# Windowed attention and a softplus feed-forward layer on one core: scores and transposes on four array tiles, the global-row picks on eight

## The chip, the cores and the metric

The kernel runs on one core of one Trainium2 chip. The metric is the device time of one execution in microseconds (us); lower is better. A core has a matrix engine (PE, with its weight loads shown apart as PEld), a vector engine (DVE), an activation engine (ACT), a general engine (POOL) and a queue engine (SP). POOL and SP also issue DMA transfers.

## The reference

```python
def _attn_ref(q, k, v, global_idx):            # q, k, v: (8, 8, 576, 64); 8 global positions
    scores = scale * np.matmul(q, k.transpose(0, 1, 3, 2))
    mask = np.abs(pos[:, None] - pos[None, :]) <= 32
    mask = mask | is_global[:, None] | is_global[None, :]
    scores = np.where(mask, scores, -1000000000.0)
    attn = softmax(scores)
    return np.matmul(attn, v)

def _moe_ref(x, w_in, w_out):                  # x: (4608, 512), d_ff 2048
    h = x @ w_in
    return softplus(h) @ w_out
```

Eight batches of eight heads with 576 positions and 64 elements a head. Each position attends to a band of 32 positions on either side and to eight global positions; the global positions attend to everything. The attention's output goes through two dense layers with a softplus between them. Inputs and outputs are float32; the kernel computes in bfloat16 with float32 sums.

## The kernel before

**Order.** Nothing runs in the order of the text. Every piece of work is a job with a cost per engine, dependencies, a rank, and the PSUM banks and buffers that it opens (`o.add`). `_Order.run` places the jobs one after another by the time at which they could start, by rank and by number, and then emits them in that order; the engines' queues follow it. It prices a change of the array's form on PE with 95 ns (`SWITCH`). `KINDS` says how many PSUM tiles of a kind may be open and how many banks must be left over, `SLOTS` the same for SBUF buffers; `OPENING` and `LATER` shift ranks by the job's name. There are eight PSUM banks.

**Loads.** `load_qk` brings q or k of one batch into 72 partitions of `qn` or `kn`, each partition with eight consecutive positions of all heads. Batch 0 is brought in parts. A later batch's load waits for the turns and picks of the batch before (`add_load`).

**Preparation of a batch** (`add_prep`). Turns: `tk` and `tq` (L533, L544) transpose 72x64 pieces on two column tiles of the array, 16 transposes for a pair of heads. `kev` and `qev` copy the results from PSUM to `kx` and `qx`. From batch 1 on, `qx` holds each head's 64 columns beside 64 columns of zeros, so `qev` makes two copies and POOL clears the zeros once (`blanks_q`). Picks: `pick` (L491) gathers the eight global rows of k and of q by matmuls with a 0/1 matrix, four 32-column tiles at once, `keep` copies them, `turn` (L502) transposes them, `fill` and `gev` copy them to `kx` and `qg`.

**Scores** (`add_scores`). A unit is 64 queries of one batch, all eight heads, nine units a batch. `sc` makes a unit's scores in two jobs of two head pairs; from batch 1 on each is a full-array matmul over both heads of a pair, thanks to the zeros (L662); in batch 0 there are two 64x64 matmuls for a pair (L667). `top` (DVE, L673) adds the mask and finds the row's minimum of the negated scores.

**Softmax and values.** `ex` (ACT) exponentiates, `su` (DVE) sums, `no` (POOL, L710) normalises to `pn`, `gc` (L714) writes the global columns' weights to `gw`. `pn` is transposed by PE (`tp`) or, for most units, by a DMA transpose on SP (`pt`). `add_global` computes the global rows (`sg`, `mx`, `gexp`, `gsum`, `tg`, `lge`, `ov`, `oz`). `add_values` makes four units' outputs at once: eight or more matmuls on 64x64 tiles for the global keys (L775), 32 for the band (L785), and `xev` copies them out.

**Dense layers** (`add_moe`). 512 tokens make a tile: 16 x 4 matmuls `first` (L819), softplus on ACT, 4 x 16 matmuls `second` (L830), copies and stores.

Of the kernel before, what the change touches and what calls it, by code (L numbers as in the profile page):

```python
# [18 lines left out]
class _Order:  # L19
# [30 lines left out]

    def closed(self, key):
        if key is None:
            return 0
        ends = [u["end"] for u in self.users[key]]
        return None if None in ends else max(ends) + self.HOP

    def room(self, opens):

        t0 = 0
        want = 0  # L60
        spare = 0
        for pool, key in opens:
            cap = self.slots.get(pool) or self.kinds[pool][0]
            was = self.opened[pool]
            if len(was) >= cap:
                t = self.closed(was[-cap])
                if t is None:
                    return None
                t0 = max(t0, t)
            if pool in self.kinds:  # L70
                want += 1
                spare = self.kinds[pool][1]
# [7 lines left out]
    def run(self, free):  # L80
# [16 lines left out]
        while ready:  # L97
            best = None
            for j in ready:
# [8 lines left out]
                for e in j["cost"]:  # L108
                    t = max(t0, free[e])
                    rank = j["rank"]  # L110
                    if e == "PE" and array != 128:
                        rank = 0 if j["array"] == array else rank + 1
# [23 lines left out]
            if e == "PE" and j["array"] != array:  # L136
                array = j["array"]
                t += self.SWITCH
# [34 lines left out]
def kernel(  # L173
# [67 lines left out]

    def load_qk(b, which, h0=0, h1=H):
# [3 lines left out]
    Q_PARTS = ((0, 0, 32), (32, G, NQ - 32))  # L246
# [15 lines left out]
    load_qk(0, 1, H // 2, H)  # L262
# [25 lines left out]
    posQ2 = temp([P, QR], FP32, "posQ2")  # L288
    count(posQ2[0:G, :], [[1, QR]], 0, QR)
    count(posQ2[G:P, :], [[1, QR]], 32 * QR, QR)  # L290
    pick_w = const([P, QR, 32], BF16, "pick")
    pick_0 = const([P, QR, 32], BF16, "pick0")
# [7 lines left out]
    qx = [const([P, HP, NJ, 2, G], BF16, f"qx{i}") for i in range(2)]  # L300
# [8 lines left out]
    def blanks_q(i):  # L309
        def edges():  # L310
            nc.gpsimd.memset(kx[i][:, :, 0, 0:WIN].bitcast(I32), 0)
            nc.gpsimd.memset(kx[i][:, :, NH5 - 1, G - WIN:G].bitcast(I32), 0)
            clear(nc.gpsimd, qg[i][:])
        return [edges] + [lambda p=p, h=h: nc.gpsimd.memset(qx[i][h * D:(h + 1) * D, p, :, 1 - h, :].bitcast(I32), 0)
                          for p in range(HP) for h in range(2)]
# [13 lines left out]
    for lo, at, n in Q_PARTS:  # L329
        nc.gpsimd.dma_start(out=qn[at:at + n, :, :],  # L330
                            in_=q[0].rearrange("h (q r) d -> q h (r d)", r=QR)[lo:lo + n])
# [50 lines left out]
    def ones_g(i):  # L382
# [3 lines left out]
        for p in range(1, HP):  # L386
            nc.vector.tensor_copy(gw[i][:, :, p, 0:2 * NG], gw[i][:, :, 0, 0:2 * NG])
# [22 lines left out]
    ST, PEB, PNB, PTB, RB = 10, 5, 8, 12, 2  # L410
    SLOTS = dict(xT=2, osb=2, st=ST, pe=PEB, pn=PNB, pt=PTB, R=RB, small=2, gk=2)
    for c in range(KF):
        SLOTS[f"g{c}"] = 1

    KINDS = dict(h=(4, 2), o=(3, 1), s=(2, 0), pick=(2, 0), gt=(1, 2), tk=(4, 0), tq=(4, 2), tk0=(1, 0), tq0=(2, 0),
                 sg=(2, 1), tg=(2, 1), ov=(1, 1), tp=(2, 0), rt=(3, 0), xo=(4, 1))
# [37 lines left out]
    def add_load(b, which, deps):  # L454
# [6 lines left out]
        early = [T.get(("t" + "qk"[which] + z, b - 1, p)) for p in range(HP) for z in ("", "b")]  # L461
        early += [T.get(("pick", b - 1, x)) for x in range(2)]
        if b:
            T["load", b, which] = [o.add({"POOL": (880, 0)}, lambda e: load_qk(b, which), deps + early, rank=0, moves=4300)]
# [9 lines left out]
    def add_prep(b, gate, rank):  # L474
# [4 lines left out]
        if b < 2:  # L479
            blanks["g"] = [T["edges", 0] if b == 0 else T["blank_q", 1]]  # L480
        XN = (qn, kn)

        def pick(e, w):
# [3 lines left out]
            parts = ((pick_w, 0, NQ),) if b or w else tuple((pick_0, at, n) for lo, at, n in Q_PARTS)  # L487
# [21 lines left out]
        def gev(e):  # L509
            for h in range(2):  # L510
                r = slice(h * D, (h + 1) * D)
                copy(e, qg[i][r, :, h * NG:(h + 1) * NG], PS["gt", b][r, 0, :, 0:NG])
        for n, w in enumerate((1, 0)):
            T["pick", b, n] = o.add({"PE": (460 * (1 if b or w else 2), 530 * (1 if b or w else 2))}, lambda e, w=w: pick(e, w),
# [12 lines left out]
        plain = qx[0][:].rearrange("c p j h q -> c p (j h q)")[:, :, 0:S]  # L527
        for p in range(HP):
# [18 lines left out]

            def kev(e, p=p):
# [7 lines left out]
            def qev(e, z=0, p=p, parts=parts):  # L556
                lo, at, n = parts[z]
                t = PS["tq", b, p, z][:].rearrange("c r (j q) -> c j q r", q=G // QR)
                if b == 0:
                    copy(e, plain[:, p, lo * QR:(lo + n) * QR].rearrange("c (j q r) -> c j q r", q=G // QR, r=QR), t)  # L560
                    return
                for h in range(2):
                    c = slice(h * D, (h + 1) * D)
                    copy(e, qx[i][c, p, :, h, :].rearrange("c j (q r) -> c j q r", r=QR), t[c])
            T["tk", b, p] = o.add(mm(QR, NQ), tk, [T["load", b, 1][b == 0 and p >= HP // 2], *gate], rank=rank, opens=[("tk" if b else "tk0", ("tk", b, p))], array=64)
            T["kev", b, p] = o.add({"ACT": (635, 720), "DVE": (800, 880)}, kev, [T["tk", b, p], *late, *blanks["g"]],
                                   rank=3, uses=[("tk", b, p)])
            for z, (lo, at, n) in enumerate(parts):
                key = ("tq", b, p, z)
                T["tqb" if z else "tq", b, p] = o.add(mm(QR, n), lambda e, z=z, f=tq: f(e, z), [T["load", b, 0][z], *gate], rank=rank + z,  # L570
                                                      opens=[("tq" if b else "tq0", key)], array=64)
                n = QR * n
                T["qevb" if z else "qev", b, p] = o.add({"ACT": act(n), "DVE": (90 + 1.2 * n, 170 + 1.2 * n)} if b == 0 else {"ACT": (1270, 1370), "DVE": (1530, 1600)},
                                                        lambda e, z=z, f=qev: f(e, z), [T["tqb" if z else "tq", b, p], *late], rank=3 + z, uses=[key])

        if b == 0:
            T["pick", 0, 1]["deps"] += [T["tqb", 0, HP - 1], T["make_pick"]]
# [3 lines left out]
    def add_global(b, gate, early):  # L581
# [24 lines left out]
        def gsum(e):  # L606
# [3 lines left out]
            nc.vector.scalar_tensor_tensor(out=rv[i][:, 0:2], in0=selg[:, 0, :], scalar=rv[i][:, 2:3], in1=selg[:, 1, :],  # L610
                                           op0=OP.mult, op1=OP.add)
# [27 lines left out]
        T["gsum", b] = o.add({"DVE": (530, 630)}, gsum, [T["gexp", b], T["select"], T.get(("oz", b - 2))], rank=2)  # L639
# [9 lines left out]
    def add_scores(n, gate, rank):  # L649
# [3 lines left out]
        def sc(e, x):  # L653
            if x == 0:
                PS["st", n] = sb.tile([P, HP, EXT], FP32, tag="st", name="st", bufs=ST)
                PS["nb", n] = sb.tile([P, HP], FP32, tag="nb", name="nb", bufs=ST)
            kf = kx[i][:].rearrange("c p a w -> c p (a w)")
            ps = PS["s", n, x] = psum(("s", n, x), [P, 2, EXT], FP32)
            for y in range(2):
                p = x * 2 + y  # L660
                if b:
                    nc.tensor.matmul(out=ps[:, y, :], lhsT=qx[i][:, p, j, :, :].rearrange("c h q -> c (h q)"),  # L662
                                     rhs=kf[:, p, j * W:j * W + EXT], start=True, stop=True)
                    continue
                for h in range(2):
                    r = slice(h * D, (h + 1) * D)
                    nc.tensor.matmul(out=ps[r, y, :], lhsT=qx[0][:].rearrange("c p j h q -> c p (j h q)")[r, p, j * G:(j + 1) * G],  # L667
                                     rhs=kf[r, p, j * W:j * W + EXT], start=True, stop=True)

        def top(e, x):  # L670
            for y in range(2):
                p = x * 2 + y
                nc.vector.tensor_tensor_reduce(out=PS["st", n][:, p, :], in0=PS["s", n, x][:, y, :], in1=mask[:, j, :],  # L673
# [372 lines left out]
```

## Time and profile before

| what | value |
|---|---|
| median of 3 runs | 372.06 us (371.8 to 889.26) |
| the profiled execution | 371.55 us, span 369.8 us |
| PE busy | 350.3 us (95% of the span) |
| DVE, ACT, POOL busy | 239.5, 277.2, 153.4 us |
| instructions | 10736 |
| granted PE clock, mean | 1.000 |

The span runs from the first to the last instruction that the profiler recorded; the execution's own time is 1.75 us longer. "Busy" counts the time in which an engine had an instruction under way. PE's matmuls are pipelined, so their records overlap: how long a group really holds PE is read from the difference between its start and that of the next group.

### The profile page before, as it was taken

Reading aid. Unit: us, or ns where it says so; the run is one execution under the profiler, and the core shown is the slowest. Engines: PE = TensorE matmul, PEld = TensorE weight load, DVE = VectorE, ACT = ScalarE, POOL = GpSimd, SP = SyncE. Lnnn points to the kernel's source line nnn. Section 1 sums busy time; section 2 is a strip of 40 time slices with the busy share of each in tenths; the row PEclk is TensorE's granted clock in tenths of the full one; section 3 lists DMA queues with packets and bytes.
Section 4 is the critical chain, followed back from the end, with each engine's and each line's share of the span. In section 5 each row is a group of like instructions: output and inputs, shape, how many; then the busy total and the mean of one; then the engine's idle time right before and its main releaser. Section 6 shows DMA issues by size and latency. Waiting matters only on the chain.

```text
span 369.8 us, 10736 instructions
## 1 busy us (share of the span) xinstructions
PE 350.3 (95%) x4044; PEld 194.3 (53%) x4044; DVE 239.5 (65%) x1028; ACT 277.2 (75%) x724; POOL 153.4 (41%) x258
## 2 busy tenths in 40 slices
PE   1977999999999999999999999999999999999996
PEld 0744777465545554555455545544554455445444
DVE  5689758996679756975697569755975595163011
ACT  3695898997599759885988598959895986784710
POOL 8988820691038503940295029502840180060000
PEclk9999999999999999999999999999999999999999
DMA  6999993099319981698159916980692022021002
GB/s 95 153 234 188 195 168 61 31 104 176 88 44 144 153 156 45 130 144 166 40 132 122 183 40 139 139 170 31 143 107 76 29 87 59 1 73 58 0 30 85
DMA packets 86164, 38.99 MB, mean 105 GB/s; under 512 B 68064, under 2 KB 79584, under 8 KB 86112
## 3 DMA queue, kind: packets, MB, share of 16 engines
q0 software_dynamic: 53248, 18.37, 46.8%
q1 hardware_dynamic: 32864, 19.94, 23.7%
q8 instruction: 31, 0.51, 0.6%
q14 instruction: 21, 0.17, 0.2%
HBM read 36.71 MB, written 9.44 MB: 125 GB/s over the span
## 4 chain that ended last, share of the span: by engine, by line
PE 68%; DVE 15%; ACT 7%; DMA 4%; issue 3%; POOL 3%; DVEq 0%; POOLq 0%; ACTq 0%
PE h L819 34%; PE o L830 16%; DVE sm L702 6%; PE s L662 4%; PE xo L785 3%; ACT pe L694 2%; PE tq L544 2%; DMA qn<-in_q_dram 2%; DVE rs L704 2%; PE pick L491 2%; DVE rs L703 2%; PE tk L533 2%; DVE osb L448 2%; PE xo L775 1%; ACT L602 1%
## 5 line engine op out<-in xcount | busy, mean ns | idle before, releaser
L710 POOL TENSOR_TENSOR pn<-pe,rs 128x512 bf16<-128x512 f32 x72 | 74.7, 1039 | 169.5 <-DVE rs L704 134.4
L819 PE MATMUL h<-xT,win 128*128 128x512 bf16 (+1 forms) x640 | 138.8, 361 | 0.1
L830 PE MATMUL o<-wout,g 128*128 128x512 bf16 (+1 forms) x592 | 136.2, 374 | 0.0
L825 ACT ACTIVATE g<-h 128x512 bf16<-128x512 f32 (+1 forms) x160 | 86.0, 558 | 41.9 <-PE h L819 40.9
L673 DVE CUSTOM_DVE_ANT_0 st<-s,mask 128x136 f32<-128x136 f32 x288 | 69.8, 295 | 45.3 <-PE s L662 43.8
L694 ACT ACTIVATE pe<-st,nb 128x136 f32<-128x136 f32 x288 | 92.1, 403 | 0.8 <-DVE nb L673 0.7
L819 PEld LDWEIGHTS <-win 128*128 128x128 bf16 x640 | 60.1, 99 | 50.9 <-issue 2.0
L830 PEld LDWEIGHTS <-g 128*128 128x128 bf16 x592 | 55.1, 98 | 57.2 <-issue 3.3
L702 DVE TENSOR_REDUCE sm<-pe 128x4 f32<-128x544 f32 x63 | 44.8, 711 | 10.0 <-ACT pe L694 9.8
L448 DVE COPY osb<-o 128x512 f32<-128x512 f32 (+1 forms) x26 | 17.3, 664 | 28.2 <-PE o L830 28.1
L251 POOL DMA_DIRECT2D vA<-in_v_dram x40 | 34.3, 874 | 0.0
L448 DVE COPY qx<-tq 64x576 bf16<-64x576 bf16 (+2 forms) x35 | 25.5, 728 | 5.6 <-PE tq L544 5.0
L662 PEld LDWEIGHTS <-qx 128*128 128x128 bf16 x252 | 20.5, 98 | 14.2 <-issue 0.3
L662 PE MATMUL s<-kx,qx 128*128 128x136 bf16 x252 | 26.9, 223 | 0.0
L673 DVE DVE_READ_ACCUMULATOR2_ANT nb<- 128x1 f32 x288 | 23.8, 83 | 0.0
L448 ACT CAST xT<-xo 128x512 bf16<-128x512 f32 x19 | 10.9, 590 | 12.1 <-PE xo L785 12.1
L533 PE MATMUL tk<-ident_b,kn 72*64 72x72 bf16 x512 | 13.5, 205 | 6.2 <-DMA kn<-in_k_dram 6.2
L448 ACT COPY kx<-tk 128x32 bf16<-128x32 bf16 (+1 forms) x75 | 18.0, 359 | 1.9 <-PE tk L533 1.8
L704 DVE TENSOR_TENSOR rs<-rs,notg 128x4 f32<-128x4 f32 x72 | 17.7, 246 | 2.5
L448 ACT COPY qx<-tq 64x576 bf16<-64x576 bf16 (+2 forms) x29 | 17.2, 593 | 1.9 <-PE tq L544 1.6
L714 POOL TENSOR_TENSOR gw<-pe,rs 128x32 bf16<-128x32 f32 x72 | 17.2, 238 | 3.0 <-DVE rs L704 1.8
L703 DVE RECIPROCAL rs<-sm 128x4 f32<-128x4 f32 x72 | 12.7, 177 | 6.5
(113 smaller groups left out, 347.5 us busy)
## 6 DMA issues: line engine op xcount, KB each, us to landing
out_dram<-osb SPq DMA_DIRECT2D x35, 256.0 KB, 2.2
vB<-vA SPq DMA_DIRECT2D x16, 256.0 KB, 7.0
kn<-in_k_dram POOLq DMA_DIRECT2D x7, 576.0 KB, 12.1
qn<-in_q_dram POOLq DMA_DIRECT2D x7, 576.0 KB, 14.6
vA<-in_v_dram POOLq DMA_DIRECT2D x24, 128.0 KB, 6.4
win<-in_moe_w_in_dram POOLq DMA_DIRECT2D x2, 1024.0 KB, 15.6
wout<-in_moe_w_out_dram POOLq DMA_DIRECT2D x4, 512.0 KB, 10.7
vA<-in_v_dram POOLq DMA_DIRECT2D x16, 96.0 KB, 5.2
```

Of the source, the lines that this page charges most:

```text
L251: nc.gpsimd.dma_start(out=vA[b % 2][p0:p0 + hi - lo, t, :].rearrange("p (h d) -> p h d", h=H), in_=SRC[2][b, :, lo:hi, :].rearrange("h s d ...
L448: (nc.scalar.copy if e == "ACT" else nc.vector.tensor_copy)(out, in_)
L533: nc.tensor.transpose(out=ps[h * D:(h + 1) * D, r, :], in_=kn[0:NQ, p * 2 + h, r * D:(r + 1) * D], identity=ident_b[0:NQ, 0:NQ])
L662: nc.tensor.matmul(out=ps[:, y, :], lhsT=qx[i][:, p, j, :, :].rearrange("c h q -> c (h q)"), rhs=kf[:, p, j * W:j * W + EXT], start=True, ...
L673: nc.vector.tensor_tensor_reduce(out=PS["st", n][:, p, :], in0=PS["s", n, x][:, y, :], in1=mask[:, j, :], scale=-SCALE, scalar=3.0e38, op0 ...
L694: nc.scalar.activation(out=pe[:, p, 0:EXT], in_=PS["st", n][:, p, :], func=AF.Exp, bias=PS["nb", n][:, p:p + 1], scale=-1.0, **({"accum_ou ...
L702: nc.vector.reduce_sum(out=sm[:], in_=PS["pe", n][:, :, 0:EXT], axis=AX)
L704: nc.vector.tensor_tensor(out=rs[:], in0=rs[:], in1=notg[:, j:j + 1].to_broadcast([P, HP]), op=OP.mult)
L710: nc.gpsimd.tensor_tensor(out=pn[:].rearrange("c p (a s) -> c p a s", a=2), in0=wide[:, :, :, 0:G], in1=rs[:].unsqueeze(2).unsqueeze(3).to ...
L819: nc.tensor.matmul(out=h[:, :], lhsT=w_in_t[c * P // WC][:, kd, c * P % WC:c * P % WC + P], rhs=PS["xT", m][:, kd, lo:hi], start=(kd == 0) ...
L825: nc.scalar.activation(out=PS["g", m, c][:, lo:hi], in_=PS[key][:, :], func=AF.Softplus)
L830: nc.tensor.matmul(out=PS[key][:, :], lhsT=PS["g", m, kf][:, ns * P:(ns + 1) * P], rhs=w_out_t[kf // 4][:, kf % 4, lo:hi], start=(kf == 0) ...
```

## The change

- Scores from batch 1 on are no longer full-array matmuls with zeros. Every unit has eight 64x64 matmuls that address four tiles of the array, and three units make one job, which opens four PSUM banks. `qx` loses its zeros, and POOL its memsets. In odd head pairs the two heads' halves of the partitions are swapped, and `gw`, `rv` and the value matmuls follow.
- From batch 1 on q and k lie in one buffer `nq`, k in partitions 0 to 63 and q in 64 to 127: eight slices of 512 positions and a ninth with the last 64. Each is loaded by two transfers (`load_main`, `load_rest`), and all four wait for every turn and pick of the batch before. One turn job (`tkq`) transposes q and k of two head pairs with 72 transposes on four tiles and opens four banks; there are two such jobs a batch.
- The picks of q and k from batch 1 on are one job of 24 matmuls on eight 64x32 tiles.
- Batch 0 loads q by heads instead of by rows, so its turns of q are whole.
- A value job may run its global part first or last, so that it meets the array's form before it.
- `gsum` makes two small operations of one. Buffers (`ST`, `PTB`), `KINDS` and the ranks are new.

```diff
+    def enters(self, j, array):
+        return 64 if j.get("both") and array == 64 else j["array"]
...
+    nq = const([P, H, (QR + 1) * D], BF16, "nq")
+    def load_main(b, which):
+        nc.gpsimd.dma_start(out=nq[(1 - which) * G:(2 - which) * G, :, 0:QR * D],
+                            in_=SRC[which][b, :, 0:G * QR].rearrange("h (q r) d -> q h (r d)", r=QR))
+    def load_rest(b, which):
+        nc.gpsimd.dma_start(out=nq[(1 - which) * G:(2 - which) * G, :, QR * D:], in_=SRC[which][b, :, G * QR:].rearrange("h q d -> q h d"))
...
-    qx = [const([P, HP, NJ, 2, G], BF16, f"qx{i}") for i in range(2)]
+    qx = [const([P, HP, S], BF16, f"qx{i}") for i in range(2)]
...
-    ST, PEB, PNB, PTB, RB = 10, 5, 8, 12, 2
+    ST, PEB, PNB, PTB, RB = 12, 5, 8, 14, 2
...
-    KINDS = dict(h=(4, 2), o=(3, 1), s=(2, 0), pick=(2, 0), gt=(1, 2), tk=(4, 0), tq=(4, 2), tk0=(1, 0), tq0=(2, 0),
-                 sg=(2, 1), tg=(2, 1), ov=(1, 1), tp=(2, 0), rt=(3, 0), xo=(4, 1))
+    KINDS = dict(h=(4, 0), o=(4, 0), s=(4, 0), pick=(4, 0), gt=(1, 2), tk=(2, 0), tq=(3, 2), tk0=(1, 0), tq0=(3, 1),
+                 sg=(3, 0), tg=(1, 1), ov=(1, 0), tp=(4, 1), rt=(4, 1), xo=(4, 1))
...
-        if b:
-            T["load", b, which] = [o.add({"POOL": (880, 0)}, lambda e: load_qk(b, which), deps + early, rank=0, moves=4300)]
+        early += [T.get(("tk", b - 1, p)) for p in range(HP) if b > 1]
+        early += [T.get(("pick", b - 1, x)) for x in range(2) if b > 1]
+        T["load", b, which] = [o.add({"POOL": (880, 0)}, lambda e: load_main(b, which), deps + early, rank=0, moves=3900),
+                               o.add({"POOL": (850, 0)}, lambda e: load_rest(b, which), deps + early, rank=0, moves=1000)]
...
+        def pick_both(e):
+            for r in range(QR + 4):
+                g = r % 4
+                for w in range(2):
+                    rows = slice((1 - w) * G, (2 - w) * G)
+                    hs = slice(0, H) if r < QR else slice(g * 2, g * 2 + 2)
+                    x = min(r, QR)
+                    nc.tensor.matmul(out=PS["pick", b, w][g * 32:(g + 1) * 32, hs, :], lhsT=pick_b[rows, x, :],
+                                     rhs=nq[rows, hs, x * D:(x + 1) * D], start=(r < 4), stop=(r >= QR))
...
+            def tkq(e, p=p):
+                for r in range(QR + 1):
+                    for w, ps in ((1, PS["tk", b, p]), (0, PS["tq", b, p, 0])):
+                        rows = slice((1 - w) * G, (2 - w) * G)
+                        for h in range(2):
+                            nc.tensor.transpose(out=ps[h * D:(h + 1) * D, r, :], in_=nq[rows, p * 2 + h, r * D:(r + 1) * D],
+                                                identity=ident_b[rows, rows])
...
-            nc.vector.scalar_tensor_tensor(out=rv[i][:, 0:2], in0=selg[:, 0, :], scalar=rv[i][:, 2:3], in1=selg[:, 1, :],
-                                           op0=OP.mult, op1=OP.add)
+            for y in range(2):
+                nc.vector.tensor_scalar(out=rv[i][:, y:y + 1], in0=rv[i][:, 2:3], scalar1=selg[:, 0, y:y + 1],
+                                        scalar2=selg[:, 1, y:y + 1], op0=OP.mult, op1=OP.add)
...
-                if b:
-                    nc.tensor.matmul(out=ps[:, y, :], lhsT=qx[i][:, p, j, :, :].rearrange("c h q -> c (h q)"),
-                                     rhs=kf[:, p, j * W:j * W + EXT], start=True, stop=True)
                 for h in range(2):
                     r = slice(h * D, (h + 1) * D)
+                    for y in range(2):
+                        c = slice((h ^ y) * G, (h ^ y) * G + G)
+                        ps, at = PS["s", u, x * 2 + y]
+                        nc.tensor.matmul(out=ps[c, at, :], lhsT=qx[i][r, x * 2 + y, ju * G:(ju + 1) * G],
+                                         rhs=kf[r, x * 2 + y, ju * W:ju * W + EXT], start=True, stop=True)
...
+        units = [n] if b == 0 else [n - j % 3 + u for u in range(3)]
...
-    OPENING = dict(blank_w=-2, first=0.5, no=0.5, oev=2, ones_g=-2, sec=4.5, su=2.5, w_in=1, w_out=-4)
-    LATER = dict(first=2, gc=-1, kev=-8, oev=-0.5, pick=2, qev=1, re=2, sec=1, sg=3, su=1.5, top=-0.5, w_out=-4)
+    OPENING = dict(gc=-5, pt=2.5, softh=4, su=2.5, top=2.5, w_out=-5)
+    LATER = dict(blank_w=-0.5, ex=-0.5, lge=3, mx=2, pick=4, qev=2, re=2.5, sc=-1.5, su=2.5, tk=-1, tp=-2, w_out=-6)
```

## The prediction

> **What bounds the kernel now.** I read the page first: spans, the slices and the chain that ended last.
>
> ```profile
> span 369.8 us, 10736 instructions
> ...
> PE 350.3 (95%) x4044; PEld 194.3 (53%) x4044; DVE 239.5 (65%) x1028; ACT 277.2 (75%) x724; POOL 153.4 (41%) x258
> ...
> PE   1977999999999999999999999999999999999996
> ...
> PE 68%; DVE 15%; ACT 7%; DMA 4%; issue 3%; POOL 3%; DVEq 0%; POOLq 0%; ACTq 0%
> ```
>
> PE is full from the fifth slice (37 us) to the end, and the chain lies on it for 68% of the span; the other engines' shares of the chain come mostly from the first 45 us. The waits of PE say how much of it is not work:
>
> ```profile
> PE tk L533 <- DMA kn<-in_k_dram: 6.2, 1, 6.2
> PE tp L720 <- POOL pn L710: 2.8, 5, 0.9
> ...
> PE xo L775 <- DVE R L448: 1.3, 4, 0.3
> ...
> PE tq L544 <- issue: 0.9, 1, 0.9
> ```
>
> Some 15 us in all, most of it before 45 us. So after the opening a microsecond taken off PE is a microsecond off the end, unless something new makes PE stand. A busy PE is not PE at its peak, so the price of each job is read from starts. The timeline of PE where a value step, turns and picks meet:
>
> ```profile
> 190.73 0.41 PE L775 MATMUL xo<-R,oz 64*64 64x256 bf16 x8 [0.34 <-DVE R L448]
> 191.07 0.22 PE L785 MATMUL xo<-pt,vB 128*64 128x64 bf16 x2
> ...
> 191.86 0.43 PE L544 MATMUL tq<-ident_b,qn 72*64 72x72 bf16 x16
> 192.12 0.69 PE L533 MATMUL tk<-ident_b,kn 72*64 72x72 bf16 x32
> 192.64 0.43 PE L544 MATMUL tq<-ident_b,qn 72*64 72x72 bf16 x16
> ...
> 193.26 0.62 PE L491 MATMUL pick<-kn,pick 72*32 72x512 bf16 x8
> ...
> 194.24 0.39 PE L830 MATMUL o<-wout,g 128*128 128x512 bf16 x1
> 194.56 0.41 PE L775 MATMUL xo<-R,oz 64*64 64x256 bf16 x8
> ...
> 197.34 1.03 PE L819 MATMUL h<-xT,win 128*128 128x512 bf16 x4
> 198.20 0.40 PE L662 MATMUL s<-kx,qx 128*128 128x136 bf16 x4
> 198.44 0.81 PE L819 MATMUL h<-xT,win 128*128 128x512 bf16 x3
> ```
>
> Differences of starts: a full matmul of 512 columns 0.216 us (four in 0.86, 197.34 to 198.20); four scores of 136 columns 0.24, 59.3 ns each; 16 turns 0.26, 16.25 ns each, so two column tiles side by side take 32.5 ns a pair; 16 picks 0.98, of which 4 x 0.216 = 0.86 is four rounds of four, and 0.12 is the change of the array's form on the way in. The full matmul at 194.24 holds 0.32: 0.216 and 0.106 for the way back. The eight matmuls of L775 on four 64x64 tiles hold 0.34: 0.12 for the form and two rounds of four at 256 columns (0.11 each). One at a time they would need 0.87. So four tiles do run together here.
>
> **The change part by part,** for the seven later batches (63 score units, PE bound):
>
> - Scores. Before 252 matmuls x 59.3 ns = 14.9 us. After 504 matmuls of 64x64, four at once: 126 rounds x 59.3 = 7.5. Gain 7.5. Bounds: all four together (0.06 a round) or only two (0.12), which would gain nothing. I take four, by L775.
> - Turns. Before 896 x 16.25 ns = 14.6 us. After nine slices instead of eight, q and k together: 1,008 transposes in 252 rounds. A round of 64 columns is not in this trace; a pair of 72 takes 32.5 ns, and 64 should be no longer: 32 ns, 8.1 us. Gain 6.5; with two at once it would be 16.1, a loss of 1.5.
> - Picks. Before 0.86 a batch; after eight tiles at once: two rounds of 512 (0.43) and one of 128 columns (0.056) = 0.49. Gain 0.375 x 7 = 2.6; with four at once 0.97, a loss of 0.8. Eight is the next size of what L775 and L491 show, so I take eight.
> - Changes of form. Scores left the full array alone; now each group of three units enters and leaves. In the two programs' order of PE instructions the form changes 123 times before and 169 after: 20 more ways in (0.12) and 26 more back (0.106): a loss of 5.1. This takes most of the scores' gain: per group three times 0.24 = 0.71 before, 0.36 + 0.23 after.
> - Sum on PE: 7.5 + 6.5 + 2.6 - 5.1 = 11.5 us.
> - Instruction supply. 8,786 rows instead of 8,090, and a turn job is now 144 instructions in 0.58 us. Before, one burst of turns stood 0.9 us on "issue" and the picks at 118 us took 0.37 more than at 193. Bounds 0 to 14 more such stops (up to 13 us); I take one more, a loss of 1.
> - Opening (first batch). DVE carries it, in the chain at 27.21 one 1.67 us instruction (L610) that becomes two short ones (like L597, 0.21): -1.3. The pick of q, in two parts, holds PE 1.9 us at 17.2, becomes one of 1.0: -0.9. Against it, k's second half is issued third (5.5 us instead of 2.3) and lands at about 10 instead of 8.1; the ten score rows of DVE (0.22 each, 2.2 us) that ran before 18 us come after it. About even; between the first two value steps more first-layer work now stands where PE waited for POOL. Gain 0.5, bounds -1.5 to +2.
> - Hidden: q evacuations in one piece instead of two 64-row halves, 56 x about 0.7 against 28 x about 0.85 us, some 15 us off DVE and ACT; 16 memsets (5.4 us) off POOL. Neither sets the end. One more kx copy per pair (28 x 0.23) stands against it.
> - Loads. Four issues a batch on POOL instead of two, 0.88 each, and they wait for both turn jobs and the picks. Behind them in POOL's queue stand the next pn products:
>
> ```profile
> 198.28 0.88 POOL L243 DMA_DIRECT2D qn<-in_q_dram  x1
> 219.38 1.03 POOL L710 TENSOR_TENSOR pn<-pe,rs 128x512 bf16<-128x512 f32 x1 [20.21 <-DVE rs L704]
> ```
>
> POOL idles 20 us there, so 1.8 us more is free (without that cover 12 us over the batches). The page gives 12.1 and 14.6 us to landing; the next turns come 30 us after the issue, and the bytes are the same, in 896 more small packets a batch. No cost. SP's queue keeps its order and count.
>
> Sum: 371.55 - 11.5 + 1.0 - 0.5 = 360.5 us, against the profiled execution (span 369.8, 1.75 around it); the median shown is 372.06, 0.5 above it. What a measurement tells from no change is about 2%, 7.4 us, so the border is 364.6.
>
> **The rivals.**
>
> A. Scores run only two at a time. Row halves of the array write into the same PSUM bank: bank A takes the upper rows' low columns and the lower rows' high columns. L775 gives each row half a bank of its own, so it does not exclude a clash. What speaks against it is the first batch before:
>
> ```profile
> 33.44 0.66 PE L667 MATMUL s<-kx,qx 64*64 64x136 bf16 x8
> 34.03 0.40 PE L819 MATMUL h<-xT,win 128*128 128x256 bf16 x1
> ```
>
> There both row halves write one bank (L667), at half pace as all of PE that early: 0.59 us for eight is 0.12 and four rounds of 0.118 (59 ns doubled), so the pairs ran together; one by one 0.95 would pass. The time by A: 360.5 + 7.5 = 368.0.
>
> [...]
>
> B. The bursts starve. If each of the 14 turn jobs stands 0.43 us for instructions, half of the worst stop above, the loss is 6: 366.5. For it: the stop on "issue" (at 82.0 us) ends just such a burst, 48 turns after 40 value matmuls. Against: at 191 to 196 some 450 instructions pass in 5.4 us without one.
>
> C. The end on the other side: banks. A score group opens four of the eight banks at once and keeps them until DVE has read twelve rows (2.6 us), a turn job four until ACT and DVE have copied them; before it was one or two. If PE stands for one softplus (0.6 us) at each of 21 + 14 jobs, 21 us are lost: 381.5. It breaks even at 0.31 us a job. Against it are ACT, which waits for h, and DVE, which waits for scores, not the reverse:
>
> ```profile
> L825 ACT ACTIVATE g<-h 128x512 bf16<-128x512 f32 (+1 forms) x160 | 86.0, 558 | 41.9 <-PE h L819 40.9
> L673 DVE CUSTOM_DVE_ANT_0 st<-s,mask 128x136 f32<-128x136 f32 x288 | 69.8, 295 | 45.3 <-PE s L662 43.8
> ```
>
> **How the numbers follow.** Forecast 0.70 (own range 356 to 364.5), A 0.08, B 0.13, C 0.09. Faster by over 2% is the forecast, 0.70; A and B lie within 2%, 0.21; C is slower, 0.09. The range takes in A and B and leaves out C; at the low end no added stop and the best opening give 358.0, and some of the 5 us that PE still waits after the opening may go too: 355.5 to 368.5.
>
> **What would show it.** Right: groups of 24 scores holding PE about 0.48 us with the way in (0.83 by A); a turn job of 72 transposes 0.6 to 0.7 (1.2 if two at once); picks 0.6; the ways back still near 0.106; the value steps from the third on coming about 1 to 1.5 us closer together per tile; the second value step (40.1 us before) at 38 to 41.5. Wrong: PE idle before scores or turns naming DVE or ACT (C), or "issue" (B); turns waiting on the nq loads, which I cost at nothing; or the value steps 37.2 us apart as before, with ACT never idle.

## The result and the profile after

| kernel | executions, us | median | ratio to the kernel before, 95% interval |
|---|---|---|---|
| before | 371.8, 372.1, 373.2 (and 889.3) | 372.6 (372.1 without the last) | 1 |
| after, first measurement | 361.7, 362.7, 367.4, 368.3 | 365.1 | 0.973 [0.967, 0.978] |
| after, second measurement (experiment 8) | 363.4 to 368.4, six | 365.9 | 0.987 [0.983, 0.990] |

The change makes the kernel faster, by 2.7% in the first measurement and 1.3% in the second. The first ratio rests on the two quicker of its four executions, because the other two, over 1.5% longer at a lower mean clock (0.990 and 0.994), were left out of it; with all four the medians stand at 0.98. What goes with that clock turned out to be the main lesson here. The second measurement is from another chip, and its ratio is to the kernel before on that chip (median 371.0). The experiments ran on several chips too, on which the kernel before has medians from 370.7 to 371.9, so a difference of 1 us between two of them says little. The profiled execution took 361.74 us (span 360.0), against 371.55 (369.8) before: 9.8 us less. The forecast was 11.0 less, 360.5.

The page of the changed kernel, the same rows as before:

```profile
span 360.0 us, 11420 instructions
...
PE 332.6 (92%) x4341; PEld 176.5 (49%) x4392; DVE 230.8 (64%) x1076; ACT 267.1 (74%) x708; POOL 156.0 (43%) x258
...
PE   2756999999998999999999999999999999999996
...
PE 63%; DVE 18%; DMA 5%; POOL 5%; ACT 4%; issue 4%; DVEq 0%; POOLq 0%; ACTq 0%; SPq 0%
```

PE is still full from 37 us on. But its share of the chain has fallen from 68% to 63%, and DVE, DMA and POOL have gained: the other engines are nearer. The one 8 among the nines, at 108 to 117 us, is the place that the experiments turn to. (The trace lacks 51 matmul records, 4341 against 4392 weight loads.) The waits of PE:

```profile
PE tk L576 <- DMA kn<-in_k_dram: 8.2, 2, 6.5
PE tp L812 <- POOL pn L802: 2.7, 2, 2.5
PE xo L883 <- DMA pt<-pn: 1.8, 3, 1.1
PE o L932 <- issue: 1.7, 11, 0.2
...
PE s L747 <- DVE nb L753: 0.4, 1, 0.4
```

No wait names `nq`, and scores wait 0.7 us in all for DVE (0.4 in the last row and 0.3 for `pt`), all of it before 45 us: rival C did not come. The eleven stops on "issue" of 0.16 us stand where a matmul record is missing; a second profile of this kernel with all 4392 records has none of them. New is the third row: the values (L883) wait 1.8 us for `pt`, the transposes by DMA, where the kernel before waited 0.5; 1.46 of it lies at one value step. PE's timeline at that place and at a score group:

```profile
109.89 0.22 PE L598 MATMUL tk<-ident_b,nq 64*64 64x64 bf16 x2
...
110.53 0.41 PE L870 MATMUL xo<-R,oz 64*64 64x128 bf16 x16
...
113.13 0.68 PE L521 MATMUL pick<-nq,pickb 64*32 64x512 bf16 x24
113.74 0.41 PE L870 MATMUL xo<-R,oz 64*64 64x256 bf16 x8
...
114.73 0.22 PE L883 MATMUL xo<-pt,vA 128*64 128x64 bf16 x2 [0.40 <-DMA pt<-pn]
116.02 0.22 PE L883 MATMUL xo<-pt,vB 128*64 128x64 bf16 x2 [1.06 <-DMA pt<-pn]
...
200.91 0.55 PE L747 MATMUL s<-kx,qx 64*64 64x136 bf16 x24
201.39 4.49 PE L921 MATMUL h<-xT,win 128*128 128x512 bf16 x19
```

By differences of starts: a turn job of 72 transposes holds PE 0.64 us (109.89 to 110.53), a pick job 0.61, a group of 24 scores 0.48 with the way in. The value step that waits, called V5 below (the second of the third tile, units 20 to 23), starts at 113.74.

The value steps are numbered V0, V1 and so on, two to a tile. From one even step to the next (V0 to V2, V2 to V4), that is tile by tile, with the work of PE beside it, an estimate summed from the prediction's prices over the two orders of instructions:

| tile | before, us | after, us | closer by | less work on PE |
|---|---|---|---|---|
| first | 45.83 | 42.49 | 3.34 | 3.04 |
| second | 37.77 | 36.06 | 1.71 | 1.01 |
| third (holds V5) | 37.84 | 36.88 | 0.96 | 1.62 |
| fourth | 37.42 | 36.38 | 1.04 | 1.12 |
| fifth | 37.23 | 35.58 | 1.65 | 1.60 |
| sixth | 37.24 | 36.85 | 0.39 | 1.02 |
| seventh | 37.36 | 37.23 | 0.13 | 0.91 |

In the whole kernel 13.1 us less work on PE (335.0 to 321.9, the first batch included) became 9.8. V5 is not the only place where some of it is lost: the sixth and seventh tile got 0.5 of their 1.9 us. In the complete profile of the second measurement PE waits there 0.8 and 0.6 us (0.5 and 0.4 on "issue" before scores, 0.3 for `pt`, 0.2 for `pn`), and before the change it waited there for nothing.

### The profile page after: what moved, and what is told of

It reads as the page before. It is cut to its first block, busy times and chain, and to the rows that moved or that the text cites. A ratio compares the mean times of both kernels' runs of the same rounds, so it can differ in the third digit from the quotient of the medians.

```text
span 360.0 us, 11420 instructions
## 1 busy us (share of the span) xinstructions
PE 332.6 (92%) x4341; PEld 176.5 (49%) x4392; DVE 230.8 (64%) x1076; ACT 267.1 (74%) x708; POOL 156.0 (43%) x258
## 4 chain that ended last, share of the span: by engine, by line
PE 63%; DVE 18%; DMA 5%; POOL 5%; ACT 4%; issue 4%; DVEq 0%; POOLq 0%; ACTq 0%; SPq 0%
PE h L921 35%; PE o L932 16%; DVE sm L794 4%; DMA pt<-pn 3%; POOL pn L802 3%; PE s L747 3%; PE xo L883 2%; DVE st L753 2%; DMA vA<-in_v_dram 2%; PE tk L598 2%; DVE osb L475 2%; DVE rs L796 2%; ACT L674 2%; DVE rs L795 2%; PE xo L870 1%
## 5 line engine op out<-in xcount | busy, mean ns | idle before, releaser
L921 PE MATMUL h<-xT,win 128*128 128x512 bf16 (+1 forms) x620 | 132.2, 361 | 1.2 <-DVE pt L475 0.2
L932 PE MATMUL o<-wout,g 128*128 128x512 bf16 (+1 forms) x561 | 129.7, 373 | 2.7 <-issue 1.7
L753 DVE CUSTOM_DVE_ANT_0 st<-s,mask 128x136 f32<-128x136 f32 x288 | 65.7, 295 | 36.7 <-PE s L747 36.6
L475 DVE COPY osb<-o 128x512 f32<-128x512 f32 (+1 forms) x31 | 20.6, 666 | 37.0 <-PE o L932 37.0
L475 ACT COPY kx<-tk 128x32 bf16<-128x32 bf16 (+2 forms) x68 | 14.7, 311 | 5.5 <-PE tk L576 2.9
L475 DVE COPY kx<-tk 128x32 bf16<-128x32 bf16 (+2 forms) x56 | 12.8, 291 | 8.6 <-PE tq L598 8.5
L747 PE MATMUL s<-kx,qx 64*64 64x136 bf16 x576 | 16.3, 235 | 1.3 <-DVE nb L753 0.4
L747 PEld LDWEIGHTS <-qx 64*64 64x64 bf16 x576 | 10.3, 110 | 12.4 <-issue 9.9
L812 PE MATMUL tp<-ident_b,pn 128*128 128x128 bf16 x96 | 10.7, 242 | 4.9 <-POOL pn L802 2.7
L883 PE MATMUL xo<-pt,vA 128*64 128x64 bf16 x320 | 12.5, 200 | 0.7 <-DMA pt<-pn 0.7
```

Source lines behind the costliest of these rows:

```text
L475: (nc.scalar.copy if e == "ACT" else nc.vector.tensor_copy)(out, in_)
L747: nc.tensor.matmul(out=ps[c, at, :], lhsT=qx[i][r, x * 2 + y, ju * G:(ju + 1) * G], rhs=kf[r, x * 2 + y, ju * W:ju * W + EXT], start=True, ...
L921: nc.tensor.matmul(out=h[:, :], lhsT=w_in_t[c * P // WC][:, kd, c * P % WC:c * P % WC + P], rhs=PS["xT", m][:, kd, lo:hi], start=(kd == 0) ...
L932: nc.tensor.matmul(out=PS[key][:, :], lhsT=PS["g", m, kf][:, ns * P:(ns + 1) * P], rhs=w_out_t[kf // 4][:, kf % 4, lo:hi], start=(kf == 0) ...
```

## The experiments

**1. Scores bank by bank.** Same instructions, another order within a group: twelve matmuls on two of the four tiles, then twelve on the other two.

```diff
-                ju = u % NJ
+            for y, u, x, ju in [(y, *z, z[0] % NJ) for y in range(2) for z in slots if z[1] in xs]:
                 for h in range(2):
...
-                    for y in range(2):
+                    if True:
```

> The changed kernel with one difference: the matmuls of a score group come bank by bank (first all of one PSUM bank, alternating the two row halves of the array, then all of the other), so that no more than two of the four 64x64 tiles can work at once; the instructions, banks, changes of form and the order of the jobs stay. Theory (four tiles at once are what the scores gain): a group of 24 goes from about 0.48 us with the way in to 0.71 + 0.12 = 0.83, the 21 groups of the later batches lose 21 x 0.36 = 7.5 us, and the first batch some 0.5 more: 361.7 + 7.5 to 8 = 369.5 us. Rival A (two row halves cannot write one PSUM bank at once): in this order every matmul would stand alone, a group 24 x 59 ns + 0.12 = 1.54 us, 21 x 1.06 = 22 us more, 384. Rival (scores are hidden and the gain came from elsewhere): no change, 361.7.

Measured: 369.28 us, ratio 0.989 [0.986, 0.993]. The group, in the timeline of PE:

```profile
200.27 0.69 PE L747 MATMUL s<-kx,qx 64*64 64x136 bf16 x24
200.90 3.63 PE L921 MATMUL h<-xT,win 128*128 128x512 bf16 x16
```

0.63 us, neither 0.83 nor 1.54. Rival A is out: row halves that write one bank do run together. My own number missed too: the order does not hold the scores to two tiles, since the second half's matmuls, on the other two tiles, begin before the first half's are done. In the trace starts come in pairs 59 ns apart, and at 200.42 us a second row of such pairs sets in beside the first, which ends at 200.59: that fits the second half starting after three of the first half's six pairs. 21 x 0.15 is 3.2 us of work; the median rose by 3.4 over the second measurement of after, on a chip where the kernel before is 0.8 slower, so the total does not tell this loss from noise (0.989 against 0.987).

**2. Turns and picks by halves.**

```diff
-                for r in range(QR + 1):
-                    for w, ps in ((1, PS["tk", b, p]), (0, PS["tq", b, p, 0])):
+                for w, ps in ((1, PS["tk", b, p]), (0, PS["tq", b, p, 0])):
+                    for r in range(QR + 1):
...
-            for r in range(QR + 4):
-                g = r % 4
-                for w in range(2):
+            for w in range(2):
+                for r in range(QR + 4):
+                    g = r % 4
```

> The changed kernel with one difference: a turn job transposes all slices of k and then all of q, and a pick job gathers k and then q, so that only one row half of the array works at a time (two tiles in turns, four in picks). Instructions, banks, changes of form and the order of the jobs stay. Theory (turns on four tiles and picks on eight are worth what the sum gave): a turn job goes from about 0.69 to 36 rounds x 32 ns + 0.12 = 1.27 us, 14 x 0.58 = 8.1 us; a pick job from 0.61 to 1.1, 7 x 0.49 = 3.4 us; together 11.5: 361.7 + 11.5 = 373.2 us, as slow as the kernel before. Rival 1 (turns ran only two at a time all along): 3.4 alone, 365. Rival 2 (both are hidden behind another engine): 361.7.

Measured: 366.97 us, ratio 0.988 [0.984, 0.992], not to be told from the second measurement of after; the 373 of the theory did not come. From the end of the work before it to its own end a turn job takes 0.97 us instead of 0.76, a pick job 0.64 instead of 0.61: 14 x 0.21 + 7 x 0.03 = 3.2 us. The total is near rival 1's 3.4, but not its parts (turns unchanged, picks 3.4), so it is not confirmed. As in the first experiment, order alone did not hold the work to half the tiles (0.97 us, against the 1.27 reckoned for two at a time), so what the turns would cost on two tiles was not measured here.

**3. Groups of one unit.**

```diff
-        units = [n] if b == 0 else [n - j % 3 + u for u in range(3)]
-        if b == 0 or j % 3 == 0:
+        units = [n]
+        if True:
```

(The scheduler's count of a group's instructions goes from 48 to 16 with it.)

> The changed kernel with score groups of one unit (8 matmuls, two banks) instead of three (24 matmuls, four banks). In the order of PE's instructions the form of the array then changes 141 times into a divided form and 104 times back, instead of 102 and 67. Theory (changes of form cost 0.12 in and 0.106 back, banks cost nothing): 39 x 0.12 + 37 x 0.106 = 8.6 us more, 370.3. Rival C (four banks opened at once make PE stand): smaller groups give banks back sooner and win back some of it, under 366, and waits of PE for DVE and ACT shrink.

Measured: 372.53 us, ratio 1.003 [1.000, 1.007], all of the gain gone.

```profile
200.03 0.31 PE L747 MATMUL s<-kx,qx 64*64 64x136 bf16 x8
200.28 1.90 PE L921 MATMUL h<-xT,win 128*128 128x512 bf16 x8
202.11 0.31 PE L747 MATMUL s<-kx,qx 64*64 64x136 bf16 x8
```

A group of eight holds 0.25 (0.12 and two rounds of 0.06), and the eight full matmuls behind it 1.83: 8 x 0.216 and 0.10 for the way back. The prices of a change of form stand, and giving banks back sooner wins nothing. Against 8.6 forecast the median rose 6.6 over the second measurement of after. Executions at full clock compare better: the middle of six here is 371.8 (371.2 to 372.8), that of the changed kernel's three 362.7, 9.1 us apart on different chips. The two profiled spans, both at full clock, are 11.1 apart.

**4. Scores alone,** with turns, picks and loads as before (one `load_qk` each, `tk`/`tq`/`pick` from `kn` and `qn`, their limits on banks as before):

```diff
-            if b:
+            if 0:
                 T["tk", b, p] = T["tk", b, p - 1] if p % 2 else o.add(
```

> The changed kernel with the turns, picks and loads of the kernel before (q and k in buffers of 72 rows, one load each, turns on two tiles, picks on four), so that of the three parts only the scores have changed; ranks as in the changed kernel. The form changes 101 times in and 58 back. The work of PE, summed from the prices of the prediction, is 330.0 us against 335.0 before and 321.9 after. Theory 1 (work on PE decides, and what stands besides it belongs to the ranks and the opening): 8.1 more than after, 369.8 us. Theory 2 (the 3 us more that PE stands after the change come from turn jobs, their banks and loads): 5 less than before, 366.6 us.

Measured: 434.36 us, ratio 1.165 [1.158, 1.172]. No theory foresaw this. From its page and its waits of PE:

```profile
PE 373.3 (86%) x4224; PEld 199.3 (46%) x4224; DVE 228.2 (53%) x1029; ACT 273.0 (63%) x699; POOL 148.8 (34%) x244
...
PEclk9999999579986998558999997579999995899999
```

```profile
PE rt L845 <- POOL gw L806: 9.6, 7, 4.1
PE tg L689 <- ACT pg L674: 9.2, 4, 3.1
...
PE tp L812 <- DVE rs L796: 4.1, 2, 3.3
```

PE stands for POOL, ACT and DVE in an order that was fitted to other work, 56 us by its waits where the changed kernel has 21. Among and after such stands the granted clock is halved, for 89 us in all (mean 0.898), so PE is busy for longer, not shorter. The question of the experiment is not answered by it.

**5 and 6. The rank tables exchanged:** the changed kernel with `OPENING` and `LATER` of before, and the kernel before with those of after.

> The changed kernel with the two rank tables (for the opening and for later work) of the kernel before; buffers, banks and the work stay. The form changes 101 times in and 68 back, as after: the work of PE is the same 321.9 us. Theory (the gain is work taken off PE, ranks only place it): within 1% of the changed kernel, 360 to 365 us. Rival (the new ranks bring a good part of the gain): 366 or more.

> The kernel before with the two rank tables of the changed kernel and nothing else. The form changes 88 times in and 47 back instead of 82 and 41: 1.35 us more work on PE. Theory (ranks only place the work): 371.6 + 1.4 = 373 us, within 2% of before. Rival (the new ranks bring a good part of the gain): 367 or less.

Measured: 380.44 us, ratio 1.025 [1.021, 1.029], and 389.48 us, ratio 1.049 [1.044, 1.055]. Both theories fall, and of the two rivals that of the first run holds: ranks are not mere placing, but the new ones are not better in themselves. Each table fits its own work, and with the other's the changed kernel loses 14.5 us against its second measurement, the kernel before 18.8. Part of both losses is the clock, halved in the profiles for 10.2 and 30.7 us (mean 0.986 and 0.960), which is 5 and 15 us of PE's work. The kernel before with the new ranks, its waits of PE:

```profile
PE rt L753 <- POOL gw L714: 7.0, 4, 3.0
PE tk L533 <- DMA kn<-in_k_dram: 6.2, 1, 6.2
PE tg L616 <- ACT pg L602: 2.5, 2, 1.5
```

**7. Scores alone with the ranks of before.**

> Only the scores of the change, with turns, picks and loads as before, and now with the two rank tables of the kernel before. The form changes 90 times in and 53 back; the work of PE sums to 328.2 us against 335.0 before and 321.9 after. Theory 1 (work on PE decides where the order is one that was fitted to nearly the same work): 371.6 - 6.8 = 364.8 us. Theory 2 (any order that was not fitted to its very work makes PE stand for 10 us or more, as in the three kernels with exchanged ranks or parts): 375 or more.

Measured: 379.48 us, ratio 1.021 [1.017, 1.025]: theory 2. The profiled execution, the longest of four (384.8 us), waits 12 us more on PE than the kernel before (27.3 against 15.5) and runs 20.5 us at half clock (mean 0.972). What the scores would bring alone in an order fitted to them stays open.

**8. The changed kernel again.** By then the run of experiment 1 had shown 4.4 us of standing at V5 and half the clock from the middle of it on.

> The changed kernel once more, unaltered, for the spread of its times. Its first four runs lie in two groups, 361.7 and 362.7 against 367.4 and 368.3. Theory (its second value step of the third tile, V5 at 114 us, waits 0 to 4 us for the last two transposes by DMA, which land late beside the loads of v for the next batch; where that wait is long, PE runs at half its clock for some 6 us afterwards, as in the run with scores bank by bank): two groups again, 361 to 363 and 366 to 369. Rival (the two slow runs were chance): one group at 361 to 363.

Measured: 365.92 us (363.4 to 368.4), ratio 0.987 [0.983, 0.990]. The ten executions of both measurements go by their mean clock: at 1.000 the times are 361.7, 362.7 and 363.4; at 0.994 to 0.995 they are 365.4, 365.7, 366.2 and 367.4; at 0.990 to 0.991 they are 367.6, 368.3 and 368.4. This profile is one of the second kind. PE at V5, and the clock behind it (the columns are the window, its length, busy time of PE, PEld, DVE, ACT and POOL, the granted clock, DMA share and GB/s):

```profile
114.35 0.22 PE L883 MATMUL xo<-pt,vA 128*64 128x64 bf16 x2
114.40 0.20 PE L883 MATMUL xo<-pt,vB 128*64 128x64 bf16 x2
116.21 0.22 PE L883 MATMUL xo<-pt,vA 128*64 128x64 bf16 x2 [1.61 <-DMA pt<-pn]
118.03 0.22 PE L883 MATMUL xo<-pt,vB 128*64 128x64 bf16 x2 [1.59 <-DMA pt<-pn]
...
119.67 4.25 PE L921 MATMUL h<-xT,win 128*128 128x512 bf16 x12
```

```profile
118.50:119.00 0.50, 0.50 (x35) 0.44 (x31) 0.50 (x1) 0.34 (x1) 0.28 (x1) 1.00 1.97 211
119.00:119.50 0.50, 0.50 (x71) 0.50 (x64) 0.10 (x1) 0.50 (x3) 0.00 (x0) 0.81 2.02 160
119.50:120.00 0.50, 0.50 (x19) 0.24 (x10) 0.38 (x2) 0.50 (x4) 0.00 (x0) 0.50 2.18 180
...
122.50:123.00 0.50, 0.50 (x3) 0.24 (x2) 0.00 (x0) 0.33 (x1) 0.30 (x1) 0.77 2.01 184
123.00:123.50 0.50, 0.50 (x4) 0.20 (x2) 0.00 (x0) 0.40 (x1) 0.00 (x0) 1.00 0.76 103
```

The clock is 0.50 from 119.31 to 122.73: 3.42 us (a clock of 0.81 in half a microsecond is 0.19 us at half). The twelve matmuls at 119.67 take 4.19 us to the next group, in the first profile 2.69. The mean clocks are steps of the same size: 3.4 us at half clock is 0.0047 of the span, twice that 0.0095. So V5 costs twice in this execution, once in standing (3.2 us) and again in clock (1.7 us of work a step). Seven of the ten executions show one or two such steps; that they too come from V5 is argued, since only this one was profiled. The kernel before has them as well, in 14 of the 59 executions measured beside these runs (0.985 to 0.995); none of them was profiled, so where it loses its clock is not known.

**9. The loads of v behind both value steps.** The first `vA` loads for the next batch are issued at 113.1 us in the first profile, while V5's last transposes are under way.

```diff
-            job["deps"] += [*held, T["ov", b - 2], T["shift", b - 2]]
+            job["deps"] += [*held, T["val", ((b - 1) * NJ - 1) // 4 | 1], T["ov", b - 2], T["shift", b - 2]]
```

> The changed kernel with one more dependence: the loads of v for a later batch wait for both value steps of a tile and not only for the last one that reads the buffer, so they start behind V5 and not 1 us ahead of it. Theory: the last transposes by DMA land 1.3 us after their issue and not 4; the wait of 1.5 us at V5 falls under 0.4, PE keeps its clock, and the runs form one group at 359.5 to 361.5. Rival 1 (the transposes are late because the products on POOL are late): the wait stays at 1 us or more, and so do the two groups. Rival 2 (v, q and k are now late): waits of PE at a turn or value step on loads, 363 or more.

Measured: 364.43 us (362.6 to 365.8), ratio 0.982 [0.979, 0.984]. Half right, and the 359.5 to 361.5 of the theory did not come:

```profile
116.17 0.22 PE L883 MATMUL xo<-pt,vA 128*64 128x64 bf16 x2 [1.53 <-DMA pt<-pn]
116.66 0.22 PE L883 MATMUL xo<-pt,vB 128*64 128x64 bf16 x2 [0.27 <-DMA pt<-pn]
```

The second wait fell from 1.59 to 0.27, so that one came from the loads, as far as one profile of each tells. The first did not (1.53), and the clock still fell to 0.50 in the profiled run, for 3.41 us (117.02 to 120.43). The transpose waited for there stands in SP's queue right behind an output store (issued at 110.83, landed at 115.01); that the store delays it is only argued. A landing 1.3 us after the issue, as the theory had it, is in none of the profiles kept: the quickest takes 2.4. And late ones are not new: in the kernel before the two transposes behind the store at 114.47 took 4.6 and 4.5 us (issued at 115.11 and 116.43), and there the first load of v was issued only at 119.32.

**10. Scores on two tiles,** in the kernel of experiment 9. Here two of the four tiles are taken away, and the order is changed so that the other two alternate.

```diff
-                for h in range(2):
-                    r = slice(h * D, (h + 1) * D)
-                    for y in range(2):
-                        c = slice((h ^ y) * G, (h ^ y) * G + G)
+                for y in range(2):
+                    for h in range(2):
+                        r = slice(h * D, (h + 1) * D)
+                        c = slice(h * G, h * G + G)
```

> The kernel with v behind both value steps, and every score matmul on one of only two tiles, upper rows with low columns and lower rows with high columns, alternating, both writing one PSUM bank (in odd head pairs the heads of the result are swapped: the kernel computes another thing there, at the same cost). Theory (two tiles at once can't be beaten here, and two row halves may write one bank): a group of 24 takes 12 rounds x 59 ns + 0.12 = 0.83 us instead of 0.48, 21 x 0.35 = 7.4 us more than the kernel with v behind both value steps, about 367.5. Rival A (row halves cannot write one bank at once): 24 x 59 ns + 0.12 = 1.54 us a group, 22 us more, 382. Rival (as in the run bank by bank, the pace is not set by the tile): 0.62 a group, 3 us more, 363.5.

Measured: 369.82 us, ratio 0.996 [0.993, 0.999]. Experiment 9 ran on the same chip: the medians are 5.4 apart and the profiled spans, each with one step of half clock, 6.6, at 7.4 forecast.

```profile
201.12 0.90 PE L747 MATMUL s<-kx,qx 64*64 64x136 bf16 x24
201.95 3.63 PE L921 MATMUL h<-xT,win 128*128 128x512 bf16 x16
```

0.83 us a group, as the theory said to the hundredth. In these groups two tiles whose rows are different halves, writing one bank, ran two at a time (0.83 us); the changed kernel's four ran four at a time (0.48).

**11. V5 behind the second turn job** (with the edit of experiment 9):

```diff
+    T["val", 5]["deps"] += [T["tk", 3, 2]]
```

> The kernel with v behind both value steps, and V5 (the second value step of the third tile) put behind the second turn job instead of ahead of it: the work of PE is the same but for one change of form less. Theory (PE stands at V5 because the last two transposes by DMA land at 116 to 117 us, and falls to half its clock when it stands there too long): V5 starts 1 us later, the wait falls from 1.8 to under 0.9, and the clock stays at 1.000 in most runs: 361 to 363 us. Rival (the half clock belongs to the load on the chip at that place and not to the wait): the clock stays at 0.995 and the time at 364 to 365.

Measured: 363.94 us (362.5 to 364.6), ratio 0.980 [0.977, 0.982]. V5 starts at 116.05 and waits 0.15 us; the clock is 1.000 in four of five executions and 0.995 in one (364.31). The rival's clock of 0.995 did not come: the work at this place is nearly the same, and the clock stays. But PE now stands 0.75 us for `gk` ahead of V5 and 0.53 for `xT` behind it, so the time is above what I expected.

**12. V5 without late transposes by DMA:** as 11, with units 22 and 23 transposed by PE behind the picks.

```diff
+    [T["tp", n]["deps"].append(T["pick", 3, 0]) for n in (22, 23)]
...
-        if n >= TURNED and (n < NN - 16 or n % 8 < 4):
+        if n >= TURNED and n not in (22, 23) and (n < NN - 16 or n % 8 < 4):
```

> As v5_behind_second_turn, and the last two of V5's transposes (units 22 and 23) are made by PE behind the picks instead of by DMA: 8 transposes of 128 columns, 0.45 us more on PE. Theory: no wait on a transpose by DMA is left at V5, and no fall of the clock; all runs in one group, 361.0 to 362.5 us, and by its interval faster than the changed kernel. Rival (the half clock belongs to the place and not to the wait): clock 0.995, 364 to 365. Rival (the products on POOL are late too): PE waits for pn at these transposes for over 1 us instead.

Measured: 362.40 us (362.1 to 365.4), ratio 0.979 [0.975, 0.982].

```profile
113.73 0.62 PE L812 MATMUL tp<-ident_b,pn 128*128 128x128 bf16 x8
114.55 0.60 PE L543 MATMUL gt<-sel,gk 128*128 128x8 bf16 x8 [0.20 <-ACT gk L475]
115.72 0.41 PE L870 MATMUL xo<-R,oz 64*64 64x256 bf16 x8
...
117.87 1.02 PE L921 MATMUL h<-xT,win 128*128 128x512 bf16 x3 [1.11 <-ACT xT L475]
```

No wait on `pt`, and the clock is 0.999 or 1.000 in all six executions, four of them at 362.1 to 362.4. The two at 364.0 and 365.4 are not explained. PE still stands there, 1.11 us for `xT` behind V5, and at full clock this version is no faster than the changed kernel (361.7, 362.7 and 363.4): what it wins is the steps of half clock. By its median it is the best version, 3.5 us below the ten executions of the changed kernel, and faster than it by its interval (0.975 to 0.982 against 0.983 to 0.990, each against the kernel before on its own chip).

## Why the prediction was right, and where not

- **Scores: right.** A group takes 0.48 us, as said, and 0.83 when held to two tiles (experiment 10), so the 7.5 us are there in the time of the jobs; at the end of the kernel experiment 10 found 5.4 to 6.6 of 7.4. Rival A, two row halves that cannot write one bank at once, would have made experiment 10's group 1.54 us; it took 0.83. The row of L667 had said so before.
- **Turns and picks: right in size.** 0.64 us a turn job (0.6 to 0.7 foreseen), which leaves 0.52 for 18 rounds, 29 ns each where I took 32; 0.61 a pick job. No experiment took tiles from them, so what they bring to the end is read from these job times alone.
- **Changes of form: right.** 0.10 back and 0.12 in, measured again in experiment 3.
- **Copies: right.** The copies of q from `tq` in the later batches fell from 39.3 to 25.0 us on DVE and ACT together, 14 where I said some 15; the added copy of k (128x64) costs 6.1, where I said 28 x 0.23 = 6.4.
- **Loads of q and k: right.** They land 13 to 17 us ahead of the turn that reads them, from the second load on.
- **Instruction supply: nothing, where I took a loss of 1.** The complete profile has 1.0 us of such stops (two before scores, 0.8, and one before a turn job, 0.2), against 0.9 before the change. B did not come.
- **Opening: about nothing, as said** (V0 at 31.98 instead of 31.87), but its parts were not: the second value step, V1, came at 41.97, outside my 38 to 41.5, and the third, V2, 3.2 us earlier than before the change.
- **Value steps: right for four tiles, wrong for two.** From the third step on I foresaw 1 to 1.5 us a tile. The second to fifth tile gave 1.0 to 1.7, the sixth and seventh 0.4 and 0.1.
- **The step that fell short** is "after the opening a microsecond taken off PE is a microsecond off the end, unless something new makes PE stand", with nothing set down for the second half. At V5 something did. PE reaches it 6.1 us sooner than before (113.74 against 119.81), and the chain of softmax, product on POOL and transpose on SP's queue was no longer ahead of it. The kernel before already waited there, so there was no slack, and I did not price it:

```profile
PE xo L785 <- DMA pt<-pn: 0.5, 1, 0.5
...
119.81 0.41 PE L775 MATMUL xo<-R,oz 64*64 64x256 bf16 x8
...
120.99 0.22 PE L785 MATMUL xo<-pt,vB 128*64 128x64 bf16 x2 [0.55 <-DMA pt<-pn]
```

  The stand at V5 grew from 0.55 to 1.46 us in the first profiled execution, and to 3.2 us with a step of half clock in the second. That is most of the gap between 360.5 and the 365.9 of the ten executions' median: with v loaded later and no late transposes at V5 (experiment 12) 3.5 of these 5.4 us are gone. The 361.7 of the first profiled execution, so near the forecast, was partly luck: its clock stayed at 1.000, as in only three of the ten. The range held all ten.
- **A term that is missing altogether** is the order. I counted the rank tables at nothing, and the new buffers and bank limits too. That was near the truth only because the new ranks fit the new work: with the old ones the kernel is slower than before (experiment 5). No rival of mine had this, and it is the one that would have turned the sign. What the buffers and bank limits bring was not measured.

## What to carry to other kernels

When work is taken off the busiest engine, look for the place where it already waits a little, even half a microsecond, for a chain on other engines: there part of what was saved ahead of it can turn into waiting. A change to a kernel whose order was fitted by hand or by search is two changes; part of it measured with the other's order measures the order. And when executions of one kernel differ by a per cent, sort them by the mean granted clock and look for the stand of PE ahead of the dip before calling it noise.

## What the runs showed of the hardware

- **A stand of PE can be paid twice.** Around 3.20 us of waiting at V5 the clock was halved for 3.42 us (experiment 8), around 1.80 for 3.41 (experiment 9), around 4.39 in experiment 1 for 6.82 (116.42 to 123.24), which is twice as long. It can last longer still: on the page of experiment 4 two slices of 10.8 us in a row have 5 tenths. What sets these lengths, and what ends them, was not looked into.
- **How long PE stood did not decide it alone.** At V5 and close by, waits of 1.46 us in the first profile, 1.43 in experiment 11 (0.75, 0.15 and 0.53) and 1.31 in experiment 12 (0.20 and 1.11) left the clock at 1.00 from 108 to 123 us; 1.80 in experiment 9, 2.27 in experiment 10, 3.20 in experiment 8 and 4.39 in experiment 1 went with half clock. But in experiment 2 PE stood only 1.15 us from 114 to 120 us (busy for 2.02 and 2.83 of two times 3.00), and the clock was 0.85 from 117 to 120 and 0.58 from 120 to 123, some 3.4 us at half. So of four stands of 1.15 to 1.46 us the shortest went with a step of half clock and the others with none, and what tells them apart was not shown.
- **Order did not keep the tiles apart.** With all matmuls of two tiles first and all of the other two after, 24 scores took 0.51 us without the way in (0.63 less 0.12, experiment 1), where four at once take 0.36 and two at once 0.71 (0.48 and 0.83 less 0.12). The later ones set in at 200.42 us, while the starts of the earlier ones went on to 200.59. To keep the scores to two tiles it took an edit that gives the other two no work (experiment 10).
